# Batch 0 by heads, first weight slices of 128 columns, and a first unit that contracts group 0 first

## The chip, the cores and the metric

The kernel runs on one core of a Trainium2 chip. The core has a matrix engine (PE), a vector engine (DVE), a scalar engine (ACT), a general engine (POOL) and a sync engine (SP). DMAs are issued here from SP's queue, from POOL's queue (the only ones in this kernel that change the type on the way, float32 to bfloat16) and, for two small stores at the end, from ACT's. All of them run on the same 16 DMA engines. Each engine works through its own instructions in the order in which they were written, and the engines wait for each other by semaphores.

The metric is the device time of one execution in microseconds (us). A single execution is also profiled; its trace gives the start and end of each instruction, who waited for whom, and what the DMA engines moved. Times in the trace count from the start of the span. A line number L298 is line 298 of the kernel before.

## The reference

There are 8 batches of 8 heads, each 576 positions by 64, then a gated feed-forward layer over 4608 tokens of 512 features.

```python
# attention without a score matrix
q_s = exp(q); q_s = q_s / sum(q_s, over the 64 features)      # the maxima cancel
k_s = exp(k); k_s = k_s / sum(k_s, over the 576 positions)
kv  = einsum('bhsd,bhse->bhde', k_s, v)                        # 64 x 64 per head
x   = einsum('bhsd,bhde->bhse', q_s, kv)                       # back to 576 x 64 per head
# x: 4608 tokens x 512 (8 heads of 64 side by side)
g   = x @ w_gate                                               # 512 -> 1536
out = (g * sigmoid(g) * (x @ w_val)) @ w_out                   # 1536 -> 512
```

All inputs and the output are float32. The kernel leaves out the maxima and computes in bfloat16 with float32 sums.

## The kernel before, in words

**Tiling.** The 8 heads of a batch are two groups `G` of four heads. One load of `q`, `k` or `v` for one group brings 128 rows with two runs of 2304 bytes each, 576 KB in all; a row holds `T` = 9 positions of two heads. `xt` holds the attention's result, turned so that the 512 features stand on partitions in `KT` = 4 blocks: blocks 0 and 1 come from group 0, blocks 2 and 3 from group 1. The feed-forward layer runs in units `m_unit(c0, n, m)` (L286): for `n` tokens from `c0` and the block `m` of 128 of the 1536 hidden columns it contracts the four blocks of `xt` with `wg` (into `g_ps`), then with `wv` (into `u_ps`); ACT applies Silu to `g_ps` (L305), and DVE multiplies by `u_ps` (L306). `o_mm` (L318) contracts the result with `wo`.

**Order.** The order of the instructions is written out by hand under a manual schedule. Batch 0's attention comes first and has almost nothing beside it. Then the 12 units of batch 0's 576 tokens run (L457), each in two parts of 320 and 256 tokens; after them batch 1's attention runs between the first `o_mm`s, and from then on chunks of 512 tokens go by with the next batch's attention mixed in. PSUM has 8 banks, taken in turn.

**Batch 0's attention** (L354 to L452). SP loads q of group 0, k of group 0, q of group 1, k of group 1 (L355). When k of group 0 has landed, POOL issues v of group 0 as one DMA and v of group 1 as two (positions 0 to 4, then 5 to 8; `BANKS`, L358 to L361), with a change to bfloat16. Then it issues the weights (L380): `wg` and `wv` in turn in slices of columns 0 to 255, 256 to 639, 640 to 1023 and 1024 to 1535, and `wo` in four slices. POOL's DMAs share one queue and start in this order. A unit `m` needs the slice that holds columns 128m to 128m+127, so m = 0 and 1 need the first pair, 2 to 4 the second, 5 to 7 the third, 8 to 11 the fourth. Batch 1's loads on SP wait for the second slice of `wo` (L454).

ACT exponentiates q in two pieces by positions (0 to 4, 5 to 8) and k whole (L373, L124). DVE sums q's exponentials per position and head (`norm_sum`, L138), takes the reciprocal (L143) and multiplies (`norm_mul`, L152). PE turns the result (`turn_pe`, L166); ACT or DVE copies it out (`turn_out`). `key_sum` (L393) sums k's exponentials by matmul, `kv_first` (L404) forms k times v, `scale_first` (L417) scales it by the key sums, `x_mm` (L213) forms x, and `x_out` casts it into `xt`. `spin` (L385) runs matmuls on zeros, which keep PE at work in the lead-in.

In the first unit (`by_part`, L294) PE finishes the first 320 tokens with all four blocks for `g_ps` and `u_ps`, and then does the other 256.

Of the kernel before, what the change touches and what calls it, by code (L numbers as in the profile page):

```python
# [8 lines left out]
FP32 = mybir.dt.float32  # L9
BF16 = mybir.dt.bfloat16  # L10
AF = mybir.ActivationFunctionType
# [4 lines left out]
def kernel(  # L16
# [10 lines left out]
    nc = tc.nc  # L27

    B, H, S, D = q.shape
# [4 lines left out]
    T = S // 64  # L34
    HSTR = S * D
# [11 lines left out]
    def bank(name):  # L47
        return psp.tile([128, 512], FP32, tag="ps", name=name)
# [13 lines left out]

    raw = {}

    def head_ap(src, b, G, t0=0, t1=T):
        return bass.AP(
            tensor=src.tensor,
            offset=src[b, 4 * G].offset + 64 * t0,
            ap=[[T * 64, 128], [2 * HSTR, 2], [1, (t1 - t0) * 64]],
        )  # L70

    def load(what, src, b, G, pieces=((0, T),), after=None):
        t_ = ld.tile([128, 2, T * 64], FP32, tag=what, name=what)
        raw[what, b, G] = t_
        last = None
        for t0, t1 in pieces:
            last = nc.sync.dma_start(out=t_[:, :, 64 * t0:64 * t1], in_=head_ap(src, b, G, t0, t1))
            if after is not None:
                tc.add_manual_dep(last.ins, after.ins.name, SYNC, reason="order of loads")
                after = None  # L80
        return last
# [34 lines left out]

    st = {}

    def exp_of(what, b, G, pieces=((0, T),)):
        s = st.setdefault((b, G), {})  # L120
        e = s["e" + what] = at.tile([128, T, 2, 64], BF16, tag="e" + what, name="e" + what)
        src = raw[what, b, G].rearrange("p h (t d) -> p t h d", d=64)
        for t0, t1 in pieces:
            nc.scalar.activation(out=e[:, t0:t1], in_=src[:, t0:t1], func=AF.Exp)  # L124

    def cast_v(b, G):
        nc.gpsimd.tensor_copy(  # L127
# [1 line left out]
            in_=raw["v", b, G].rearrange("p h (t d) -> p t h d", d=64),  # L129
        )  # L130

    def norm_sum(b, G, pieces=((0, T),)):
        s = st[b, G]
        eq2 = s["eq"].rearrange("p t h d -> p (t h) d")
        rs = at.tile([128, 2 * T], FP32, tag="rs", name="rs")
        first = None
        for t0, t1 in pieces:
            i = nc.vector.reduce_sum(  # L138
                out=rs[:, 2 * t0:2 * t1], in_=eq2[:, 2 * t0:2 * t1, :], axis=mybir.AxisListType.X
            )  # L140
            first = first or i
        rr = s["rr"] = at.tile([128, 2 * T], FP32, tag="rr", name="rr")
        nc.vector.reciprocal(out=rr, in_=rs)  # L143
        return first

    def norm_mul(b, G, pieces=((0, T),), engs=None):
        s = st[b, G]
        eq2 = s["eq"].rearrange("p t h d -> p (t h) d")
        qs = s["qs"] = at.tile([128, T, 128], BF16, tag="qs", name="qs")
        for (t0, t1), eng in zip(pieces, engs or (nc.vector, nc.vector)):  # L150
            n = 2 * (t1 - t0)
            eng.tensor_mul(  # L152
                qs[:, t0:t1, :].rearrange("p t (h d) -> p (t h) d", d=64),
                eq2[:, 2 * t0:2 * t1, :],
                s["rr"][:, 2 * t0:2 * t1].to_broadcast([128, n, 64]),
            )
# [78 lines left out]
    def x_one(b, G):  # L235
        for i in range(2):
            x_out(b, G, i, x_mm(b, G, i))
# [45 lines left out]

    def m_unit(c0, n, m, by_part=False):  # L286
        ms = slice(m * 128, (m + 1) * 128)
        parts = [(c0, n)] if n <= 512 else [(c0, 320), (c0 + 320, n - 320)]
        gu = []
        for nm in ("g_ps", "u_ps"):  # L290
            ps = [bank(nm) for _ in parts]
            gu.append(ps)
        steps = [(a, kk, i) for a in range(2) for kk in range(KT) for i in range(len(parts))]
        if by_part:  # L294
            steps.sort(key=lambda a: (a[2], a[0], a[1]))
        for a, kk, i in steps:
            c, w_ = parts[i]
            nc.tensor.matmul(  # L298
                out=gu[a][i][:, 0:w_], lhsT=(wg, wv)[a][:, kk, ms], rhs=xt[:, kk, c:c + w_],
                start=(kk == 0), stop=(kk == KT - 1),  # L300
            )
        for g_ps, u_ps, (c, w_) in zip(gu[0], gu[1], parts):
            r = c % RING
            sg = ff.tile([128, 512], BF16, tag="sg", name="sg")
            nc.scalar.activation(out=sg[:, 0:w_], in_=g_ps[:, 0:w_], func=AF.Silu)  # L305
            nc.vector.tensor_mul(hr[:, m, r:r + w_], sg[:, 0:w_], u_ps[:, 0:w_])  # L306
# [46 lines left out]
    with tc.manual_schedule():  # L353
        kd = []  # L354
        for G in range(NG):  # L355
            load("q", q, 0, G)
            kd.append(load("k", k, 0, G))
        d = nc.gpsimd.dma_start(out=v16[0], in_=head_ap(v, 0, 0))  # L358
        tc.add_manual_dep(d.ins, kd[0].ins.name, SYNC, reason="order of loads")
        for t0, t1 in BANKS:  # L360
            nc.gpsimd.dma_start(out=v16[1][:, :, 64 * t0:64 * t1], in_=head_ap(v, 0, 1, t0, t1))  # L361

        warm = const.tile([128, 1], FP32, name="warm", tag="warm")
        nc.vector.memset(warm, 0.0)
# [5 lines left out]
        for vb in vbs:  # L370
            nc.vector.memset(vb[:, :, 128:129], 1.0)

        exp_of("q", 0, 0, BANKS)  # L373
        exp_of("k", 0, 0)
        exp_of("q", 0, 1, BANKS)
        first = norm_sum(0, 0, BANKS)
        norm_mul(0, 0, BANKS)
        norm_sum(0, 1, BANKS)

        for c0, n in ((0, 256), (256, 384), (640, 384), (1024, 512)):  # L380
            w_slice(wg, moe_w_gate, c0, n)
            w_slice(wv, moe_w_val, c0, n)
        w_dma = [wo_slice(m0, 3) for m0 in (0, 3, 6, 9)]

        def spin(n, after=None):  # L385
            idle = bank("idle")
            for _ in range(n):
                i = nc.tensor.matmul(out=idle, lhsT=zero[:, 0:128], rhs=zero, start=True, stop=True)  # L388
                if after is not None:
                    tc.add_manual_dep(i.ins, after.ins.name, SYNC, reason="start of the warm-up")  # L390
                    after = None

        def key_sum(G):  # L393
            s = st[0, G]
            ks = bank("ks")
            for t in range(T):
                nc.tensor.matmul(
                    out=ks[:, 0:2], lhsT=s["ek"][:, t, :, :].rearrange("p h d -> p (h d)"), rhs=sel,
                    start=(t == 0), stop=(t == T - 1),
                )  # L400
            s["kvr"] = at.tile([128, 2], FP32, tag="kvr", name="kvr")
            nc.vector.reciprocal(out=s["kvr"], in_=ks[:, 0:2])

        def kv_first(G, t0=0, t1=T):  # L404
            s = st[0, G]
            if t0 == 0:
                s["kv"] = [bank("kv") for _ in range(2)]
            for t in range(t0, t1):
                for g in range(2):
                    r = slice(64 * g, 64 * g + 64)  # L410
                    nc.tensor.matmul(
                        out=s["kv"][g][:, 0:128].rearrange("p (h d) -> p h d", d=64),
                        lhsT=ek_of(0, G, g, t), rhs=v16[G][r, :, 64 * t:64 * t + 64],
                        start=(t == 0), stop=(t == T - 1),
                    )

        def scale_first(G, eng1):  # L417
            s = st[0, G]
            kn = s["kn"] = at.tile([128, 2, 128], BF16, tag="kn1", name="kn1")
            nc.scalar.mul(kn[:, 0, :], s["kv"][0][:, 0:128], s["kvr"][:, 0:1])  # L420
            if eng1 is nc.scalar:
                nc.scalar.mul(kn[:, 1, :], s["kv"][1][:, 0:128], s["kvr"][:, 1:2])
            else:
                nc.vector.tensor_scalar_mul(kn[:, 1, :], s["kv"][1][:, 0:128], s["kvr"][:, 1:2])

        spin(8)
        spin(6, first)
        key_sum(0)
        turn_pe(0, 0, 0)
        turn_pe(0, 0, 1)  # L430
        turn_out(0, 0, 0, nc.scalar)
        exp_of("k", 0, 1)
        turn_out(0, 0, 1, nc.scalar)
        norm_mul(0, 1, BANKS)
        spin(6)
        key_sum(1)
        kv_first(0)
        scale_first(0, nc.scalar)
        turn_pe(0, 1, 0)
        turn_pe(0, 1, 1)  # L440
        turn_out(0, 1, 0, nc.vector)
        turn_out(0, 1, 1, nc.vector)
        xp0 = x_mm(0, 0, 0), x_mm(0, 0, 1)
        kv_first(1, *BANKS[0])
        kv_first(1, *BANKS[1])
        x_out(0, 0, 0, xp0[0], (nc.scalar, nc.scalar))
        x_out(0, 0, 1, xp0[1], (nc.vector, None))
        scale_first(1, nc.vector)
        xp1 = x_mm(0, 1, 0), x_mm(0, 1, 1)
        x_out(0, 1, 0, xp1[0], (nc.scalar, nc.vector))  # L450
        x_out(0, 0, 1, xp0[1], (None, nc.vector))
        x_out(0, 1, 1, xp1[1], (nc.scalar, nc.vector))  # L452

        load_batch(1, w_dma[-3], by_group=True)  # L454
        load_batch(2)

        for m in range(MT):  # L457
            m_unit(0, S, m, by_part=(m == 0))

        exp_of("q", 1, 0)  # L460
        exp_of("k", 1, 0)
# [121 lines left out]
```

The softmax here doesn't subtract the row's maximum and nothing guards it: scores larger than these inputs give would overflow.

## Time and profile before

Five runs took 317.33 to 317.72 us, with a median of 317.46.

| | |
|---|---|
| profiled execution, its own time | 317.2 us |
| its span | 315.3 us |
| granted clock of PE | 1.0 throughout |
| PE busy | 306.7 us (97%), 1894 matmuls |
| DVE, ACT, POOL busy | 163.0, 147.5, 28.1 us |
| PE busy from 0.00 to 6.40 us | 3.60 us, all of it zeros |
| PE busy from 6.40 to 14.40 us (batch 0's attention) | 6.93 us |
| PE busy from 14.40 to 17.04 us (first unit) | 2.31 us |
| PE busy from 17.04 to 38.60 us (the other 11 units) | 21.56 us, all of it |
| DMA's mean rate from 17.04 to 38.60 us | 234 GB/s |

PE is busy almost everywhere after 17 us, so a microsecond that the lead-in loses or wins before that point goes into the whole time, unless a later wait takes it back. For a DMA, the profile gives when it was issued and how long after that it landed. The rate of a DMA that changes the type is counted in the bytes that it writes, half of those that it reads.

### The profile page before, as it was taken

What the parts mean: (1) busy time and instruction counts of PE and PEld (TensorE: products, weight loads), DVE (VectorE), ACT (ScalarE), POOL (GpSimd) and SP (SyncE); (2) the same over time, 40 slices, a digit from 0 to 9 for tenths busy, and PEclk for the clock granted to TensorE, in tenths of its full rate; (3) what the DMA queues carried; (4) which work ended last, traced back from release to release, by engine and by line L of the source; (5) the groups of instructions that cost most, each with busy time, mean ns of one, the idle gap of its engine ahead of it and who ended that gap; (6) DMA issues with size and microseconds to landing.
All of it is one profiled execution on the core that took longest, in us unless ns stands there. A gap on an engine that the chain in (4) does not pass through costs nothing.

```text
span 315.3 us, 4885 instructions
## 1 busy us (share of the span) xinstructions
PE 306.7 (97%) x1894; PEld 152.0 (48%) x1894; DVE 163.0 (52%) x277; ACT 147.5 (47%) x218; POOL 28.1 (9%) x35
## 2 busy tenths in 40 slices
PE   6899999999999999999999999999999999999994
PEld 2477744554444444544454444444454444444443
DVE  3834485784854566455835492639354333423421
ACT  4843488534673475447454737455743113312300
POOL 2920021101100110002000200020000000000000
PEclk9999999999999999999999999999999999999999
DMA  7999999278337815590639153944310202020124
GB/s 275 189 203 207 304 392 389 64 180 338 64 77 201 317 25 119 129 388 2 141 73 377 68 119 64 323 156 104 70 36 0 68 1 67 0 69 5 29 69 102
DMA packets 39305, 45.75 MB, mean 145 GB/s; under 512 B 16369, under 2 KB 23025, under 8 KB 39281
## 3 DMA queue, kind: packets, MB, share of 16 engines
q1 hardware_dynamic: 32480, 39.99, 42.1%
q0 software_dynamic: 6640, 5.31, 10.9%
q8 instruction: 15, 0.25, 0.3%
q10 hardware_dynamic: 160, 0.13, 0.2%
q14 instruction: 10, 0.07, 0.1%
HBM read 37.75 MB, written 9.44 MB: 150 GB/s over the span
## 4 chain that ended last, share of the span: by engine, by line
PE 92%; DMA 3%; ACT 1%; DVE 1%; POOL 1%; issue 0%; SPq 0%
PE g_ps L298 30%; PE u_ps L298 29%; PE o_ps L322 27%; PE kv L191 3%; DMA wv<-in_moe_w_val_dram 2%; DMA k<-in_k_dram 2%; PE xp L267 1%; PE o_ps L342 1%; POOL v L361 0%; DVE qs L152 0%; DVE rs L138 0%; PE tp L166 0%; ACT L124 0%; ACT eq L124 0%; POOL v L358 0%
## 5 line engine op out<-in xcount | busy, mean ns | idle before, releaser
L305 ACT ACTIVATE sg<-g_ps 128x512 bf16<-128x512 f32 (+2 forms) x120 | 65.1, 554 | 138.9 <-PE g_ps L298 131.8
L306 DVE TENSOR_TENSOR hr<-sg,u_ps 128x512 bf16<-128x512 bf16 (+2 forms) x120 | 74.4, 630 | 87.6 <-PE u_ps L298 83.0
L298 PE MATMUL g_ps<-xt,wg 128*128 128x512 bf16 (+2 forms) x480 | 111.6, 358 | 0.2 <-ACT xt L111 0.2
L298 PE MATMUL u_ps<-xt,wv 128*128 128x512 bf16 (+2 forms) x480 | 111.2, 358 | 0.3 <-DMA wv<-in_moe_w_val_dram 0.3
L322 PE MATMUL o_ps<-wo,hr 128*128 128x512 bf16 x420 | 93.6, 379 | 0.0
L298 PEld LDWEIGHTS <-wv 128*128 128x128 bf16 x480 | 46.8, 98 | 47.0 <-DMA wv<-in_moe_w_val_dram 0.6
L298 PEld LDWEIGHTS <-wg 128*128 128x128 bf16 x480 | 45.8, 98 | 45.2 <-issue 0.9
L322 PEld LDWEIGHTS <-hr 128*128 128x128 bf16 x420 | 40.9, 98 | 49.1
L113 DVE COPY o_sb<-o_ps 128x512 f32<-128x512 f32 x33 | 22.4, 680 | 39.2 <-PE o_ps L322 39.2
L127 POOL CAST vb<-v 128x1152 bf16<-128x1152 f32 x14 | 16.1, 1148 | 173.8 <-DMA v<-in_v_dram 85.0
L138 DVE TENSOR_REDUCE rs<-eq 128x18 f32<-128x1152 bf16 (+2 forms) x18 | 21.7, 1215 | 12.7 <-ACT eq L124 12.7
L152 DVE TENSOR_TENSOR qs<-eq,rr 128x1152 bf16<-128x1152 bf16 (+2 forms) x18 | 22.1, 1238 | 0.1
L124 ACT ACTIVATE eq<-q 128x1152 bf16<-128x1152 f32 (+2 forms) x18 | 18.2, 1053 | 4.0 <-DMA q<-in_q_dram 3.9
L124 ACT ACTIVATE ek<-k 128x1152 bf16<-128x1152 f32 x16 | 18.0, 1159 | 0.3 <-DMA k<-in_k_dram 0.2
L305 ACT ACT_TABLE_LOAD x12 | 15.4, 1283 | 0.2
L124 ACT ACT_TABLE_LOAD x11 | 14.1, 1283 | 0.2
L388 PE MATMUL idle<-zero 128*128 128x512 bf16 x20 | 6.5, 480 | 2.8 <-DVE rs L138 1.6
L191 PE MATMUL kv<-vb,ek 64*128 64x129 bf16 x252 | 8.7, 217 | 0.0
L191 PEld LDWEIGHTS <-ek 64*128 64x128 bf16 x252 | 7.3, 94 | 2.7 <-ACT sg L305 2.1
L275 ACT CAST xt<-xp 128x512 bf16<-128x512 f32 x12 | 6.4, 589 | 3.6 <-PE xp L267 3.6
L276 DVE CAST xt<-xp 128x512 bf16<-128x512 f32 x12 | 7.7, 682 | 0.0
L347 ACT COPY o_sb<-o_ps 128x128 f32<-128x128 f32 x2 | 0.5, 266 | 13.3 <-DVE o_sb L346 13.3
(46 smaller groups left out, 70.1 us busy)
## 6 DMA issues: line engine op xcount, KB each, us to landing
q<-in_q_dram SPq DMA_DIRECT2D x16, 576.0 KB, 5.2
k<-in_k_dram SPq DMA_DIRECT2D x16, 576.0 KB, 7.1
out_dram<-o_sb SPq DMA_DIRECT2D x70, 128.0 KB, 2.4
v<-in_v_dram SPq DMA_DIRECT2D x14, 576.0 KB, 8.8
wo<-in_moe_w_out_dram POOLq DMA_DIRECT2D x4, 384.0 KB, 16.8
wg<-in_moe_w_gate_dram POOLq DMA_DIRECT2D x2, 384.0 KB, 9.1
wv<-in_moe_w_val_dram POOLq DMA_DIRECT2D x2, 384.0 KB, 10.1
wg<-in_moe_w_gate_dram POOLq DMA_DIRECT2D x1, 512.0 KB, 13.1
```

Source lines behind the costliest of these rows:

```text
L113: eng.tensor_copy(out=out, in_=in_)
L124: nc.scalar.activation(out=e[:, t0:t1], in_=src[:, t0:t1], func=AF.Exp)
L127: nc.gpsimd.tensor_copy(out=vbs[G][:, :, 0:128].rearrange("p t (h d) -> p t h d", d=64), in_=raw["v", b, G].rearrange("p h (t d) -> p t h ...
L138: i = nc.vector.reduce_sum(out=rs[:, 2 * t0:2 * t1], in_=eq2[:, 2 * t0:2 * t1, :], axis=mybir.AxisListType.X)
L152: eng.tensor_mul(qs[:, t0:t1, :].rearrange("p t (h d) -> p (t h) d", d=64), eq2[:, 2 * t0:2 * t1, :], s["rr"][:, 2 * t0:2 * t1].to_broadca ...
L191: nc.tensor.matmul(out=kv[g][:, c:c + 129], lhsT=ek_of(b, G, g, t), rhs=vbs[G][r, t, 0:129], start=(t == 0), stop=(t == T - 1),)
L276: nc.vector.tensor_copy(out=xt[:, 2 * G + 1, c0:c0 + 512], in_=main[G][1])
L298: nc.tensor.matmul(out=gu[a][i][:, 0:w_], lhsT=(wg, wv)[a][:, kk, ms], rhs=xt[:, kk, c:c + w_], start=(kk == 0), stop=(kk == KT - 1),)
L305: nc.scalar.activation(out=sg[:, 0:w_], in_=g_ps[:, 0:w_], func=AF.Silu)
L306: nc.vector.tensor_mul(hr[:, m, r:r + w_], sg[:, 0:w_], u_ps[:, 0:w_])
L322: nc.tensor.matmul(out=o_ps, lhsT=hr[:, m, r0:r0 + 128], rhs=wo[:, m, :], start=(m == 0), stop=(m == MT - 1),)
L388: i = nc.tensor.matmul(out=idle, lhsT=zero[:, 0:128], rhs=zero, start=True, stop=True)
```

## The change

- `load` and `exp_of` take q of batch 0 head by head: two DMAs of 288 KB for each group in place of one of 576 KB, and two exponentials over 9 positions of one head each, in place of pieces by positions. `norm_sum` sums head by head in the same way.
- v of group 1 comes as one DMA, and `kv_first` of group 1 is one piece.
- The weights' columns are sliced 0 to 127, 128 to 255, 256 to 511, 512 to 1023 and 1024 to 1535: ten DMAs in place of eight.
- The order in the lead-in: `turn_pe` before `key_sum` for group 0, both of group 0's `turn_out`s before k's exponential of group 1, eight matmuls on zeros in place of six, half of group 1's turn before `kv_first(0)`, `scale_first` always on ACT and DVE together, and `x_out` always split between ACT and DVE.
- The first unit does blocks 0 and 1 for all four banks first, then blocks 2 and 3.

```diff
-    def load(what, src, b, G, pieces=((0, T),), after=None):
+    def load(what, src, b, G, after=None, by_head=False):
...
-        for t0, t1 in pieces:
-            last = nc.sync.dma_start(out=t_[:, :, 64 * t0:64 * t1], in_=head_ap(src, b, G, t0, t1))
+        for h in ((0, 1), (1, 2)) if by_head else ((0, 2),):
+            last = nc.sync.dma_start(out=t_[:, h[0]:h[1], :], in_=head_ap(src, b, G, h))
...
-        for t0, t1 in pieces:
-            nc.scalar.activation(out=e[:, t0:t1], in_=src[:, t0:t1], func=AF.Exp)
+        for h in (slice(0, 1), slice(1, 2)) if by_head else (slice(0, 2),):
+            nc.scalar.activation(out=e[:, :, h], in_=src[:, :, h], func=AF.Exp)
...
-        if by_part:
-            steps.sort(key=lambda a: (a[2], a[0], a[1]))
+        if first:
+            steps.sort(key=lambda a: (a[1] // 2, a[2], a[0], a[1]))
...
-        d = nc.gpsimd.dma_start(out=v16[0], in_=head_ap(v, 0, 0))
-        tc.add_manual_dep(d.ins, kd[0].ins.name, SYNC, reason="order of loads")
-        for t0, t1 in BANKS:
-            nc.gpsimd.dma_start(out=v16[1][:, :, 64 * t0:64 * t1], in_=head_ap(v, 0, 1, t0, t1))
+        for G in range(NG):
+            d = nc.gpsimd.dma_start(out=v16[G], in_=head_ap(v, 0, G))
+            if G == 0:
+                tc.add_manual_dep(d.ins, kd[0].ins.name, SYNC, reason="order of loads")
...
-        for c0, n in ((0, 256), (256, 384), (640, 384), (1024, 512)):
+        for c0, n in ((0, 128), (128, 128), (256, 256), (512, 512), (1024, 512)):
             w_slice(wg, moe_w_gate, c0, n)
             w_slice(wv, moe_w_val, c0, n)
...
         spin(8)
         spin(6, first)
+        turn_pe(0, 0, 0)
         key_sum(0)
-        turn_pe(0, 0, 0)
         turn_pe(0, 0, 1)
         turn_out(0, 0, 0, nc.scalar)
+        turn_out(0, 0, 1, nc.scalar)
         exp_of("k", 0, 1)
-        turn_out(0, 0, 1, nc.scalar)
         norm_mul(0, 1, BANKS)
-        spin(6)
+        spin(8)
+        turn_pe(0, 1, 0)
+        kv_first(0)
+        turn_out(0, 1, 0, nc.vector)
+        scale_first(0)
+        turn_pe(0, 1, 1)
         key_sum(1)
-        kv_first(0)
-        scale_first(0, nc.scalar)
-        turn_pe(0, 1, 0)
-        turn_pe(0, 1, 1)
-        turn_out(0, 1, 0, nc.vector)
         turn_out(0, 1, 1, nc.vector)
         xp0 = x_mm(0, 0, 0), x_mm(0, 0, 1)
...
+        x_out(0, 0, 0, xp0[0])
+        kv_first(1)
+        scale_first(1)
+        x_out(0, 0, 1, xp0[1])
+        x_one(0, 1)
...
         for m in range(MT):
-            m_unit(0, S, m, by_part=(m == 0))
+            m_unit(0, S, m, first=(m == 0))
```

More of the change, by code (lines that the diff above doesn't have):

```diff
@@ L63, with head_ap @@
     raw = {}
-    def head_ap(src, b, G, t0=0, t1=T):
+    def head_ap(src, b, G, h=(0, 2)):
         return bass.AP(
             tensor=src.tensor,
-            offset=src[b, 4 * G].offset + 64 * t0,
-            ap=[[T * 64, 128], [2 * HSTR, 2], [1, (t1 - t0) * 64]],
+            offset=src[b, 4 * G + 2 * h[0]].offset,
+            ap=[[T * 64, 128], [2 * HSTR, h[1] - h[0]], [1, T * 64]],
         )
-    def load(what, src, b, G, pieces=((0, T),), after=None):
+    def load(what, src, b, G, after=None, by_head=False):
         t_ = ld.tile([128, 2, T * 64], FP32, tag=what, name=what)
@@ L117, with exp_of @@
     st = {}
-    def exp_of(what, b, G, pieces=((0, T),)):
+    def exp_of(what, b, G, by_head=False):
         s = st.setdefault((b, G), {})
@@ L130, in cast_v, with norm_sum, norm_mul @@
         )
-    def norm_sum(b, G, pieces=((0, T),)):
+    def norm_sum(b, G, by_head=False):
         s = st[b, G]
-        eq2 = s["eq"].rearrange("p t h d -> p (t h) d")
-        rs = at.tile([128, 2 * T], FP32, tag="rs", name="rs")
+        rs = at.tile([128, T, 2], FP32, tag="rs", name="rs")
         first = None
[L137 to L140, printed above, removed]
+        for h in (slice(0, 1), slice(1, 2)) if by_head else (slice(0, 2),):
+            i = nc.vector.reduce_sum(out=rs[:, :, h], in_=s["eq"][:, :, h, :], axis=mybir.AxisListType.X)
             first = first or i
         rr = s["rr"] = at.tile([128, 2 * T], FP32, tag="rr", name="rr")
-        nc.vector.reciprocal(out=rr, in_=rs)
+        nc.vector.reciprocal(out=rr, in_=rs.rearrange("p t h -> p (t h)"))
         return first
-    def norm_mul(b, G, pieces=((0, T),), engs=None):
+    def norm_mul(b, G, pieces=((0, T),)):
         s = st[b, G]
@@ L149, in norm_mul @@
         qs = s["qs"] = at.tile([128, T, 128], BF16, tag="qs", name="qs")
-        for (t0, t1), eng in zip(pieces, engs or (nc.vector, nc.vector)):
+        for t0, t1 in pieces:
             n = 2 * (t1 - t0)
-            eng.tensor_mul(
+            nc.vector.tensor_mul(
                 qs[:, t0:t1, :].rearrange("p t (h d) -> p (t h) d", d=64),
@@ L282, in x_both, with m_unit @@
             )
-    def m_unit(c0, n, m, by_part=False):
+    def m_unit(c0, n, m, first=False):
         ms = slice(m * 128, (m + 1) * 128)
@@ L355 @@
         for G in range(NG):
-            load("q", q, 0, G)
+            load("q", q, 0, G, by_head=True)
             kd.append(load("k", k, 0, G))
-        d = nc.gpsimd.dma_start(out=v16[0], in_=head_ap(v, 0, 0))
-        tc.add_manual_dep(d.ins, kd[0].ins.name, SYNC, reason="order of loads")
-        for t0, t1 in BANKS:
-            nc.gpsimd.dma_start(out=v16[1][:, :, 64 * t0:64 * t1], in_=head_ap(v, 0, 1, t0, t1))
+        for G in range(NG):
+            d = nc.gpsimd.dma_start(out=v16[G], in_=head_ap(v, 0, G))
+            if G == 0:
+                tc.add_manual_dep(d.ins, kd[0].ins.name, SYNC, reason="order of loads")
         warm = const.tile([128, 1], FP32, name="warm", tag="warm")
@@ L371 @@
             nc.vector.memset(vb[:, :, 128:129], 1.0)
-        exp_of("q", 0, 0, BANKS)
+        exp_of("q", 0, 0, True)
         exp_of("k", 0, 0)
-        exp_of("q", 0, 1, BANKS)
-        first = norm_sum(0, 0, BANKS)
+        exp_of("q", 0, 1, True)
+        first = norm_sum(0, 0, True)
         norm_mul(0, 0, BANKS)
-        norm_sum(0, 1, BANKS)
-        for c0, n in ((0, 256), (256, 384), (640, 384), (1024, 512)):
+        norm_sum(0, 1, True)
+        for c0, n in ((0, 128), (128, 128), (256, 256), (512, 512), (1024, 512)):
             w_slice(wg, moe_w_gate, c0, n)
@@ L402, in key_sum, with kv_first @@
             nc.vector.reciprocal(out=s["kvr"], in_=ks[:, 0:2])
-        def kv_first(G, t0=0, t1=T):
+        def kv_first(G):
             s = st[0, G]
-            if t0 == 0:
-                s["kv"] = [bank("kv") for _ in range(2)]
-            for t in range(t0, t1):
+            s["kv"] = [bank("kv") for _ in range(2)]
+            for t in range(T):
                 for g in range(2):
@@ L415, in kv_first, with scale_first @@
                     )
-        def scale_first(G, eng1):
+        def scale_first(G):
             s = st[0, G]
@@ L420, in scale_first @@
             nc.scalar.mul(kn[:, 0, :], s["kv"][0][:, 0:128], s["kvr"][:, 0:1])
[L421 to L424, printed above, removed]
+            nc.vector.tensor_scalar_mul(kn[:, 1, :], s["kv"][1][:, 0:128], s["kvr"][:, 1:2])
         spin(8)
         spin(6, first)
+        turn_pe(0, 0, 0)
         key_sum(0)
-        turn_pe(0, 0, 0)
         turn_pe(0, 0, 1)
         turn_out(0, 0, 0, nc.scalar)
+        turn_out(0, 0, 1, nc.scalar)
         exp_of("k", 0, 1)
-        turn_out(0, 0, 1, nc.scalar)
         norm_mul(0, 1, BANKS)
-        spin(6)
-        key_sum(1)
-        kv_first(0)
-        scale_first(0, nc.scalar)
-        turn_pe(0, 1, 0)
-        turn_pe(0, 1, 1)
-        turn_out(0, 1, 0, nc.vector)
+        spin(8)
[4 more added lines that the diff above has]
+        turn_pe(0, 1, 1)
+        key_sum(1)
         turn_out(0, 1, 1, nc.vector)
         xp0 = x_mm(0, 0, 0), x_mm(0, 0, 1)
[L444 to L452, printed above, removed]
+        x_out(0, 0, 0, xp0[0])
[3 more added lines that the diff above has]
+        x_one(0, 1)
         load_batch(1, w_dma[-3], by_group=True)
```

## The prediction

> **What bounds the kernel now.** I read the busy shares first, then PE in order of time through the lead-in, then the landing of each weight slice, then the rate of the DMA engines. The page's busy table gives the frame:
>
> ```profile
> PE 306.7 (97%) x1894; PEld 152.0 (48%) x1894; DVE 163.0 (52%) x277; ACT 147.5 (47%) x218; POOL 28.1 (9%) x35
> ```
>
> PE is the bound, and all that the change touches lies before 25 us. So the question is when PE gets into its even step of units, and whether anything stops it there later. PE in order of time (start, length, what it does; in brackets its idle time and what ended it):
>
> ```profile
> 12.36 0.61 PE L220 MATMUL xp<-qt,kn 64*64 64x320 bf16 x8
> 12.90 0.68 PE L411 MATMUL kv<-v,ek 64*128 64x128 bf16 x18
> 14.03 0.45 PE L220 MATMUL xp<-qt,kn 64*64 64x320 bf16 x8 [0.46 <-DVE kn L424]
> ...
> 15.62 0.72 PE L298 MATMUL u_ps<-xt,wv 128*128 128x320 bf16 x4 [0.30 <-DMA wv<-in_moe_w_val_dram]
> 16.17 0.60 PE L298 MATMUL g_ps<-xt,wg 128*128 128x256 bf16 x4
> 16.61 0.60 PE L298 MATMUL u_ps<-xt,wv 128*128 128x256 bf16 x4
> 17.04 1.14 PE L298 MATMUL g_ps<-xt,wg 128*128 128x320 bf16 x8
> ...
> 22.92 1.14 PE L298 MATMUL g_ps<-xt,wg 128*128 128x320 bf16 x8
> 23.90 1.14 PE L298 MATMUL u_ps<-xt,wv 128*128 128x320 bf16 x8
> 24.88 1.14 PE L298 MATMUL g_ps<-xt,wg 128*128 128x320 bf16 x8
> 25.86 1.14 PE L298 MATMUL u_ps<-xt,wv 128*128 128x320 bf16 x8
> ```
>
> From 17.04 a unit takes 1.96 us (0.98 for `g_ps`, 0.98 for `u_ps`) without a gap. The first unit began at 14.41 and ended at 17.04, 2.63 us: 0.67 us of it is waiting, for x of group 1 and for the first `wv` slice. Counting on, m = 4 begins at 22.92 and reads `wv` from 23.90; m = 5 reads `wv` from 25.86. These two times decide what follows.
>
> The DMA issues give size and time from issue to landing, here for the first `wg`, the first `wv` and the third `wv` slice (columns 640 to 1023):
>
> ```profile
> wg<-in_moe_w_gate_dram POOLq DMA_DIRECT2D x1, 256.0 KB, 5.4
> ```
> ```profile
> wv<-in_moe_w_val_dram POOLq DMA_DIRECT2D x1, 256.0 KB, 6.0
> ```
> ```profile
> 12.48 0.79 POOL L99 DMA_DIRECT2D wv<-in_moe_w_val_dram  x1
> ```
> ```profile
> wv<-in_moe_w_val_dram POOLq DMA_DIRECT2D x1, 384.0 KB, 11.3
> ```
>
> They were issued at 8.79, 9.54 and 12.48, so they landed at 14.2, 15.5 and 23.8. The last is needed at 25.86: 2.1 us to spare. The DMA engines' packets (one per run of columns) in the single microseconds from 9, 12, 19, 26 and 63:
>
> ```profile
> DMA packets 177, 0.20 MB, mean 197 GB/s; under 512 B 5, under 2 KB 177, under 8 KB 177
> ```
> ```profile
> DMA packets 372, 0.19 MB, mean 188 GB/s; under 512 B 5, under 2 KB 372, under 8 KB 372
> ```
> ```profile
> DMA packets 272, 0.21 MB, mean 205 GB/s; under 512 B 5, under 2 KB 272, under 8 KB 272
> ```
> ```profile
> DMA packets 206, 0.21 MB, mean 210 GB/s; under 512 B 1, under 2 KB 206, under 8 KB 206
> ```
> ```profile
> DMA packets 815, 0.21 MB, mean 209 GB/s; under 512 B 815, under 2 KB 815, under 8 KB 815
> ```
>
> The first is v. The next three are slices of 256, 384 and 512 columns, written as packets of 512, 768 and 1024 bytes; the last is a transposing DMA inside the chip, in packets of 256 bytes. The weight stream is never idle up to 36 us, so a slice lands when the bytes and packets ahead of it are through; when POOL issues it hardly matters. A slice is 512 packets whatever its width: 1.38 us at 256 columns (512/372), 1.88 at 384, 2.49 at 512.
>
> **The change, part by part.**
>
> *Attention of batch 0 (all estimates from the trace's durations).* Halves of q let the first exponential start when the first 288 KB are in, some 0.8 us before the 4.78 of now; the second waits for the same landing as now, and of 576 elements per row it takes about 0.67 us (mean of 736 ns for 640 and 612 ns for 512). Thus q's exponentials end near 5.45 instead of 6.03, and DVE's sums, reciprocals and products come 0.6 to 0.75 us earlier for both groups. That gain doesn't pass on whole: `kv_first(0)` needs v of group 0, landed at 10.7 (issued 6.51, 4.2 to land), and goes at about 10.9 instead of 11.14. `scale_first` on two engines instead of ACT twice saves another 0.2: `x_mm` of group 0 at 12.0 (now 12.36). `kv_first(1)` follows at 12.5 (now 12.90), if its v is in; `x_mm` of group 1 at 13.6 (now 14.03); the first unit at 14.05 (now 14.41). The other moves cost nothing there: two more matmuls on zeros (0.43 us) end near 10.0, with group 1's products due at 10.55; group 0's second `turn_out`, now ahead of k's exponential on ACT, lets that start near 9.5, and k landed at 9.37 (issued 2.27, 7.1 to land); SP's two extra issues, 0.5 us each, delay k of group 1, whose packets run only after q's, from about 7 us.
>
> *First unit.* With blocks 0 and 1 first, PE has 0.98 us of work that needs x of group 0 alone, while group 1's casts (four of 0.38 to 0.49 us on two engines) finish by 14.8. If the first pair of slices is in, the unit takes 1.96 us and ends at 16.0: 1.0 us earlier than now. The Silu table load (1.28 us) ends by about 16.0 and holds up no PE work, since the banks of m = 0 are next needed at m = 2.
>
> *v of group 1 in one DMA.* Its two pieces landed 2.0 us after group 0's (8.1 + 4.6 against 6.51 + 4.2). As 256 packets like group 0's, 0.295 MB written at 197 GB/s, it takes 1.5: everything behind it gains 0.5.
>
> *Slices.* Up to the end of the third `wv` slice the stream was 2 x 1.38 + 4 x 1.88 = 10.28 us. Now it is four slices of 128 columns, 2 x 1.38 and 2 x 2.49 = 7.74, plus 4d, where d is the time of 512 packets of 256 bytes. No DMA of the trace shows d. From below: 0.63 us, the transposes' 815 packets per us, which is also the byte rate of the widest slices. From above: 1.38, as long as a slice of twice the width. A straight line through 2.49, 1.88 and 1.38 gives 0.88, but the rate in bytes falls already, 210, 205, 188, more at each step. The nearest row is the 256-column slice, the same queue and cast, so I go above the line, to the middle: **d = 1.0**. Change of the stream: 4.0 + 7.74 - 10.28 - 0.50 = +0.96 us (bounds -0.5 and +2.5).
>
> The first pair lands in time (14.2 - 0.5 - 0.4 = 13.3, and 15.5 - 0.5 - 0.8 = 14.2). But the new third wide slice holds columns 512 to 1023, and PE wants it at m = 4, no longer at m = 5. It lands at 23.8 + 0.96 = **24.75**; PE would want it at 16.0 + 3 x 1.96 + 0.98 = 22.9, so PE stands still about 1.9 us there, and `u_ps` of m = 4 starts 0.85 later than the 23.90 of now. Behind this wait ACT and DVE only wait along. The earlier microsecond is therefore lost, and so is any error of the attention's estimate up to 1.9 us. POOL's issue of that slice comes near 13.5, far ahead of its packets; it now waits for v of group 1 to land (12.2), which costs nothing for the same reason.
>
> *Afterwards.* The fourth pair follows in 2 x 2.49 us, needed 7.8 us later. Batch 1's loads wait for the second `wo` slice and shift by the same 0.96; its first q is read at 39.74 and landed at 38.25 (issued 32.95, 5.3 to land), and both shift alike. PE has no slack later to win it back.
>
> **Sum:** +0.85 us. The profiled execution took 317.2 around its span of 315.3, 0.26 under the median of 317.46; it becomes 318.05, and the median **318.3**. What this kernel's runs can tell from no change is about 0.2%, 0.63 us.
>
> [...]
>
> **The rivals.**
>
> *Packets cost only their bytes.* For it: 205 to 210 GB/s from 768 bytes up, and the transposes. Against it: 188 at 512. With d from 0.63 to 0.88 the sum is -0.6 to +0.4. This is the one that ends on the other side: the same wait, at m = 4 for `wv`, decides, and below d = 0.79 the kernel is faster; at 0.63 by 0.6 us, 316.8.
>
> *Small packets take as long as those of twice the size, or longer.* For it: the fall at 512 bytes. Against it: from 768 to 512 the time per packet still fell by a quarter. From d = 1.25: +1.85; at 1.38, +2.4, 319.8.
>
> *No wait at m = 4 at all*, so that the gain of the first unit stays: -1.0, 316.4. The stream would have to be 1.9 us shorter than I have it; even d = 0.63 gives only 1.5.
>
> *The attention by heads is late.* It costs only beyond the 1.9 us that the wait covers; nothing in the trace comes near.
>
> **How the numbers follow.** Forecast (d 0.88 to 1.25, +0.4 to +1.85): 50%. Bytes only: 25%. Long packets: 17%. No wait: 5%. Late attention: 3%. Faster by over 0.2%: no wait and the very end of bytes only, 0.08. Within 0.2%: most of bytes only and the forecast below d = 0.95, 0.33. Slower: 0.59. The range, 317.1 to 319.9, runs from d = 0.70 to d = 1.40 and leaves out a tenth on each side.
>
> **What would show it.** Right: the first unit ends by 16.5; PE waits for DMA `wv` at m = 4 for 1 to 3 us, ending near 24.75; about 500 packets per us while the narrow slices run; an earlier end of q's sums that moves nothing. Wrong: no DMA wait on PE after 17 us, packets over 700 per us, or a first unit that ends later than now.

## The result and the profile after

| | before | changed |
|---|---|---|
| median | 317.51 us (43 runs) | 319.39 us (24 runs) |
| lowest to highest | 317.11 to 318.94 | 317.06 to 322.19 |
| profiled execution, span | 317.2, 315.3 | 317.24, 315.3 |

The changed kernel is slower: ratio 1.0056, with an interval of 1.0041 to 1.0071, about 1.8 us. The ratio leaves out the two longest executions of the changed kernel (322.03 and 322.19), which lie over 1.5% above its fastest. The middle half of its executions spans 2.4 us, against 0.5 before, and the profiled one is among its fastest. So this profile shows the mechanism of the waits, but not the loss; that needed a profile of a typical execution, which the first experiment brought.

The page's busy table of the profiled execution is nearly that of before:

```profile
PE 306.8 (97%) x1896; PEld 152.1 (48%) x1896; DVE 163.3 (52%) x278; ACT 147.3 (47%) x217; POOL 28.8 (9%) x36
```

PE in order of time, with the instructions that answer to those shown of before, and behind them what the weight loads (PEld) waited for up to 60 us: us in total, times, longest:

```profile
11.40 0.45 PE L163 MATMUL tp<-ident,qs 128*128 128x128 bf16 x5 [1.51 <-DVE qs L149]
...
13.05 0.44 PE L217 MATMUL xp<-qt,kn 64*64 64x320 bf16 x8
13.42 0.68 PE L407 MATMUL kv<-v,ek 64*128 64x128 bf16 x18
14.55 0.45 PE L217 MATMUL xp<-qt,kn 64*64 64x320 bf16 x8 [0.45 <-DVE kn L417]
14.94 0.45 PE L295 MATMUL g_ps<-xt,wg 128*128 128x320 bf16 x2
...
16.91 1.14 PE L295 MATMUL g_ps<-xt,wg 128*128 128x320 bf16 x8
...
22.79 1.14 PE L295 MATMUL g_ps<-xt,wg 128*128 128x320 bf16 x8
24.07 1.15 PE L295 MATMUL u_ps<-xt,wv 128*128 128x320 bf16 x8
```
```profile
PEld L295 <- DMA wv<-in_moe_w_val_dram: 0.4, 1, 0.4
```

The first unit runs without a gap, 14.94 to 16.91, in 1.97 us, as forecast (1.96). But it starts later than before (14.41), where I had 14.05, and ends 0.13 us earlier than before, where I had 1.0. From 22.79 to 24.07 `g_ps` of m = 4 takes 1.28 us in place of 0.98: 0.30 us of standing still for `wv`, in the place that the prediction named, and `u_ps` starts 0.17 us later than before (24.07 against 23.90).

The DMA rate in the microsecond from 13, when only the narrow slices run, then the issues of group 0's and group 1's v and of the `wv` slice for m = 4 to 7 (size, time to landing; issued at 6.38, 7.24 and 13.63):

```profile
DMA packets 720, 0.18 MB, mean 178 GB/s; under 512 B 720, under 2 KB 720, under 8 KB 720
```
```profile
v<-in_v_dram POOLq DMA_DIRECT2D x1, 288.0 KB, 5.5
```
```profile
v<-in_v_dram POOLq DMA_DIRECT2D x1, 288.0 KB, 6.1
```
```profile
wv<-in_moe_w_val_dram POOLq DMA_DIRECT2D x1, 512.0 KB, 10.4
```

720 packets of 256 bytes per us make a 128-column slice 0.71 us, less than my 1.0. v, on the other hand, landed at 11.9 and 13.35, where before it was there at 10.7 and 12.7, and I had counted on 10.7 and 12.2. The slice itself landed at 24.03, forecast 24.75.

### The profile page after: what moved, and what is told of

Its sections match the earlier page's. It is cut to its first block, busy times and chain, and to the rows that moved or that the text cites. A ratio compares the mean times of both kernels' runs of the same rounds, so it can differ in the third digit from the quotient of the medians.

```text
span 315.3 us, 4893 instructions
## 1 busy us (share of the span) xinstructions
PE 306.8 (97%) x1896; PEld 152.1 (48%) x1896; DVE 163.3 (52%) x278; ACT 147.3 (47%) x217; POOL 28.8 (9%) x36
## 3 DMA queue, kind: packets, MB, share of 16 engines
q0 software_dynamic: 7424, 5.31, 11.2%
## 4 chain that ended last, share of the span: by engine, by line
PE 89%; DMA 7%; ACT 1%; DVE 1%; issue 0%; POOL 0%; SPq 0%
PE g_ps L295 28%; PE u_ps L295 28%; PE o_ps L319 27%; DMA wv<-in_moe_w_val_dram 3%; PE kv L188 3%; DMA v<-in_v_dram 2%; DMA k<-in_k_dram 1%; PE xp L264 1%; PE o_ps L339 1%; DVE qs L149 0%; DVE rs L137 0%; PE tp L163 0%; ACT L124 0%; ACT eq L124 0%; POOL v L356 0%
## 5 line engine op out<-in xcount | busy, mean ns | idle before, releaser
L137 DVE TENSOR_REDUCE rs<-eq 128x18 f32<-128x1152 bf16 (+1 forms) x18 | 21.8, 1215 | 12.6 <-ACT eq L124 12.6
L124 ACT ACTIVATE eq<-q 128x1152 bf16<-128x1152 f32 (+1 forms) x18 | 18.4, 1054 | 3.1 <-DMA q<-in_q_dram 2.9
## 6 DMA issues: line engine op xcount, KB each, us to landing
wg<-in_moe_w_gate_dram POOLq DMA_DIRECT2D x2, 512.0 KB, 10.7
wv<-in_moe_w_val_dram POOLq DMA_DIRECT2D x2, 512.0 KB, 12.2
```

Of the source, the lines that this page charges most:

```text
L124: nc.scalar.activation(out=e[:, :, h], in_=src[:, :, h], func=AF.Exp)
L137: i = nc.vector.reduce_sum(out=rs[:, :, h], in_=s["eq"][:, :, h, :], axis=mybir.AxisListType.X)
```

## Experiments

Each was timed over several executions beside the kernel before on the same chip. In the first four the kernel before had a median of 317.41, in the next four 317.52, in the last four 317.50. The last four ran on another chip than the first eight.

### 1. The changed kernel again

No edit.

> The changed kernel itself, once more, to see a second profile of it and how its executions scatter. Wait theory (the third wide wv slice lands late, PE stands still at m = 4): the granted clock is 1.0 and the time follows the landing of that slice, 317.2 to 319. Clock theory (PE has too little work before group 1's turn, where it waits 1.5 us for qs, so in some executions its granted clock falls for some microseconds): the executions' mean clock lies between 0.987 and 1.0, and each 0.01 of it costs about 3.2 us; the slowest are those of the lowest clock, up to 322.

321.12 us (318.99 to 322.22, 6 runs), ratio 1.0101 [1.0072, 1.0130]. The mean granted clock was 0.987, 0.987, 0.988, 0.988, 0.994 and 1.0, the last in the shortest execution; those of the kernel before lay at 0.997 or above. That is the clock theory's forecast. The profile is now of a typical execution (321.12, span 319.2). ACT's exponential of k of group 0, first in the kernel before, then here, and PE:

```profile
6.23 1.16 ACT L124 ACTIVATE ek<-k 128x1152 bf16<-128x1152 f32 x1 [0.20 <-DMA k<-in_k_dram]
```
```profile
7.29 1.16 ACT L124 ACTIVATE ek<-k 128x1152 bf16<-128x1152 f32 x1 [2.24 <-DMA k<-in_k_dram]
```
```profile
11.69 0.45 PE L163 MATMUL tp<-ident,qs 128*128 128x128 bf16 x5 [0.83 <-DVE qs L149]
...
14.82 1.14 PE L407 MATMUL kv<-v,ek 64*128 64x128 bf16 x18 [1.16 <-DMA v<-in_v_dram]
16.42 0.71 PE L217 MATMUL xp<-qt,kn 64*64 64x320 bf16 x8 [0.46 <-DVE kn L417]
17.06 0.71 PE L295 MATMUL g_ps<-xt,wg 128*128 128x320 bf16 x2
...
20.87 1.37 PE L295 MATMUL g_ps<-xt,wg 128*128 128x320 bf16 x8
```

And its busy times by stretch, where the number after POOL's is PE's granted clock:

```profile
5.30:14.40 9.10, 6.11 (x76) 3.27 (x74) 7.04 (x15) 5.23 (x8) 6.78 (x9) 1.00 1.04 222
14.50:21.30 6.80, 6.02 (x44) 3.77 (x45) 2.11 (x6) 3.43 (x7) 4.80 (x7) 0.50 1.44 188
21.40:40.00 18.60, 18.60 (x154) 14.85 (x153) 7.57 (x19) 6.62 (x19) 0.37 (x1) 1.00 1.20 228
```

Two losses can be read here. k of group 0 is exponentiated at 7.29, not at 6.23 as before; v waits for that landing to be issued at all; group 1's v holds PE up until 14.82 (before: 12.90). And from 14.5 to 21.3 the matrix engine ran at half its clock: the first unit takes 3.81 us in place of 1.96. PE's 18 matmuls of `kv` took 1.14 us in place of 0.68. No wait for `wv` is left at m = 4 here, because PE is later than the slice. The trace's clock record has the half clock for 6.83 us in this execution. In the other three profiles with a fall (runs 3, 11 and 12) it lasts 3.41, 3.41 and 6.83 us, and the four falls come at different times: 14.49 here, then 13.28, 7.57 and 14.75. PE was not idle in the 3.41 us before the fall here: it was busy for 1.97 us between 11.07 and 14.49, and its longest gap was 1.2 us.

### 2. More matmuls on zeros

```diff
         norm_mul(0, 1, BANKS)
-        spin(8)
+        spin(14)
         turn_pe(0, 1, 0)
```

> The changed kernel with 14 instead of 8 matmuls on zeros before group 1's turn, 1.3 us more, which fills PE's 1.5 us of waiting. Clock theory: the granted clock stays at 1.0 in nearly every execution and the median falls from 319.4 to 317.5 or 318. Wait theory: PE waits at m = 4 as before, the median stays near 319.

319.21 us (318.31 to 319.85, 8 runs), ratio 1.0048 [1.0031, 1.0064]; the clock was at 0.997 or above in all eight. Beside it the changed kernel had 321.12 (six executions), and 319.39 in the 24 of the result, so what goes with the clock is 0.2 to 1.9 us by these medians. Among those 24, the 13 executions with a clock of 0.997 or above have a median of 318.64, the other 11 one of 321.14; they may differ in more than the clock. The clock recovers, as the clock theory said, but its 317.5 to 318 was missed: 1.8 us over the kernel before remain. The wait theory's 319 came true for another reason. In this run's profile PE waits for v of group 0 until 13.23, and the first unit starts at 16.45; the wait at m = 4 is again 0.3 us. So most of the rest is neither that wait nor the clock, but late v.

### 3. The old slices in the changed kernel

```diff
-        for c0, n in ((0, 128), (128, 128), (256, 256), (512, 512), (1024, 512)):
+        for c0, n in ((0, 256), (256, 384), (640, 384), (1024, 512)):
```

> The changed kernel with the column slices of the kernel before (256, 384, 384, 512), all else changed. Wait theory: no wait for wv after the first unit, so the first unit's gain stays and the median is 316.5 to 317.2. Clock theory: the clock scatters as in the changed kernel (0.987 to 1.0), since the lead-in on PE is the same; the median stays 1 us or more above 317.5, near 318.5.

319.89 us (317.76 to 320.89, 8 runs), ratio 1.0070 [1.0046, 1.0095], clocks from 0.988 to 1.0. The wait theory's 316.5 to 317.2 fell. The first unit starts at 17.78, since v of group 0 lands at 13.4 and PE waits for it. So most of the loss isn't in the slices.

### 4. The new slices in the kernel before

```diff
-        for c0, n in ((0, 256), (256, 384), (640, 384), (1024, 512)):
+        for c0, n in ((0, 128), (128, 128), (256, 256), (512, 512), (1024, 512)):
```

> The kernel before with the new column slices (128, 128, 256, 512, 512), nothing else. Wait theory: with 0.74 us for a slice of 128 columns (as the profile of the changed kernel shows) the third wide wv slice lands about 24.2 and PE waits for it at m = 4, +0.3 us, up to +1.5 in executions where it lands later. Clock theory: the lead-in on PE is that of the kernel before, so the clock stays at 1.0 and nothing of the scatter up to 322 appears: 317.5 to 318.2.

317.96 us (317.42 to 318.49, 12 runs), ratio 1.0012 [1.0001, 1.0022], clocks from 0.997. This is the prediction's own mechanism by itself. In its profile the first unit ends at 16.47, 0.57 us earlier than before, and all of that goes at m = 4:

```profile
22.35 1.14 PE L298 MATMUL g_ps<-xt,wg 128*128 128x320 bf16 x8
23.90 1.15 PE L298 MATMUL u_ps<-xt,wv 128*128 128x320 bf16 x8 [0.41 <-DMA wv<-in_moe_w_val_dram]
```

`u_ps` starts at 23.90, to the hundredth as before. This profile is of the fastest execution (317.42), in which wait and gain cancel; the median is half a microsecond longer. So the mechanism is there. That the wait is longer in the other executions, and makes up the 0.5 us, is likely but not shown.

### 5. q by heads in the kernel before

```diff
-            load("q", q, 0, G)
+            load("q", q, 0, G, by_head=True)     # two DMAs, one head's run of each row in each
```

> The kernel before with one thing changed: q of batch 0 loaded head by head, two DMAs of 288 KB per group (the exponentials stay by positions). Head theory (six loads in place of four make k of group 0, or v behind it, land later on the slowest DMA engine): v of group 0 lands after 11.5 in place of 10.7, the matmuls of k times v start late, and the median rises to 318 to 320, with executions whose clock falls. Whole-v theory (it is v of group 1 as one DMA that delays v): nothing of this, 317.4 within 0.3.

319.45 us (317.17 to 321.62, 12 runs), ratio 1.0062 [1.0037, 1.0087], with clocks down to 0.987 in the three longest. This one edit gives as much loss (1.93 us) and as much scatter (middle half 2.6 us) as the whole change, and the head theory's forecast holds. The DMA engines' packets from 5 to 6 us, first in the kernel before, then here:

```profile
DMA packets 184, 0.39 MB, mean 387 GB/s; under 512 B 16, under 2 KB 16, under 8 KB 184
```
```profile
DMA packets 118, 0.24 MB, mean 237 GB/s; under 512 B 15, under 2 KB 15, under 8 KB 118
```

The queue isn't short of issued loads then: all six, 2.4 MB, had been issued by 3.6 us. Nor do the DMA engines stand idle: their busy share is 1.04 before and 1.13 here, so a packet took some 150 ns in place of 90. The stream falls to 0.6 of its rate, k of group 0 is first read at 7.28, and PE follows:

```profile
11.95 0.38 PE L402 MATMUL ks<-sel,ek 128*128 128x2 bf16 x9 [1.26 <-ACT ek L129]
12.98 0.68 PE L416 MATMUL kv<-v,ek 64*128 64x128 bf16 x18 [0.65 <-DMA v<-in_v_dram]
...
15.85 0.45 PE L225 MATMUL xp<-qt,kn 64*64 64x320 bf16 x8 [0.45 <-DVE kn L429]
16.23 0.90 PE L303 MATMUL g_ps<-xt,wg 128*128 128x320 bf16 x4
```

The first unit starts at 16.23 in place of 14.41. In the changed kernel's own two profiles the same microsecond moved 251 and 260 GB/s, in runs 2 and 3 it moved 336 and 309, and in the seven profiles with q whole 362 to 401. The dip alone doesn't say when k lands: ACT reads k of group 0 at 6.05 to 6.30 with q whole, at 6.10 in the fast profile of the result in spite of its dip, and at 6.78 to 7.98 in the other five with q by heads.

### 6. q whole in the changed kernel

```diff
-            load("q", q, 0, G, by_head=True)
+            load("q", q, 0, G)
```

> The changed kernel with q of batch 0 loaded whole again, two runs in one DMA (the exponentials stay by head). Head theory: v of group 0 lands near 10.7 again, the clock stays at 1.0 and the median falls from about 320 to 317.3 to 318.2; what is left over the kernel before is the wait for wv at m = 4, 0.3 to 0.5 us. Whole-v theory: v lands as late as in the changed kernel, median 319 or more.

317.87 us (317.50 to 318.89, 11 runs), ratio 1.0009 [1.0000, 1.0019], clock 1.0 in every execution. This is the counterpart of the last: from 5 to 6 us the rate is 378 GB/s, v of group 0 lands at 10.77. What is left over the kernel before is 0.35 us, with a wait for `wv` at m = 4 (until 24.57) and v of group 1 landing at 13.8. The head theory's forecast holds.

### 7. q whole and the old slices in the changed kernel

```diff
-            load("q", q, 0, G, by_head=True)
+            load("q", q, 0, G)
...
-        for c0, n in ((0, 128), (128, 128), (256, 256), (512, 512), (1024, 512)):
+        for c0, n in ((0, 256), (256, 384), (640, 384), (1024, 512)):
```

> The changed kernel with q loaded whole and the column slices of the kernel before. Head theory together with the wait theory: neither late v nor a wait at m = 4 is left, so the new order of the lead-in and the new first unit show what they are worth: 316.5 to 317.2. Whole-v theory: 318.5 or more.

318.33 us (317.71 to 319.04, 12 runs), ratio 1.0020 [1.0011, 1.0029]. A miss: without the wait at m = 4 it is slower, not faster, than with it, and the median lies between the two theories' ranges. The old first `wv` slice lands late, and the first unit stops for it:

```profile
15.41 0.45 PE L295 MATMUL g_ps<-xt,wg 128*128 128x320 bf16 x2
16.45 0.44 PE L295 MATMUL u_ps<-xt,wv 128*128 128x320 bf16 x2 [0.60 <-DMA wv<-in_moe_w_val_dram]
```

Here the narrow slices win 0.46 us (317.87 against 318.33), while in the kernel before they lose 0.5. That their sign depends on how late v, ahead of them in the queue, leaves the DMA engines would fit both, but no run isolates it.

### 8. v of group 1 whole in the kernel before

```diff
-        for t0, t1 in BANKS:
-            nc.gpsimd.dma_start(out=v16[1][:, :, 64 * t0:64 * t1], in_=head_ap(v, 0, 1, t0, t1))
+        nc.gpsimd.dma_start(out=v16[1], in_=head_ap(v, 0, 1))
```

> The kernel before with one thing changed: v of group 1 as one DMA. Whole-v theory: v of group 0 or of group 1 lands 1 us or more later than before (10.7 and 12.7), median 318 or more. Head theory: v of group 1 lands at 12.2 to 12.7, and the median stays within 0.3 of 317.4.

318.12 us (317.75 to 318.43, 11 runs); all eleven lie above the median of the kernel before, though the interval of the ratio, 1.0007 [0.9996, 1.0019], still reaches 1. The median is in the whole-v theory's range. In its profile v of group 1, issued at 7.18, landed at 13.45 (6.3 us), against 12.68 before. One DMA in place of two is later, not earlier. In the changed order it is the same: 13.83 in run 6 with one DMA, 13.0 in run 9 with two. In this profile PE never waits for v itself, but the first `wv` slice behind it is late too, and the first unit, which before went on at 15.62, stops for it:

```profile
16.37 0.72 PE L298 MATMUL u_ps<-xt,wv 128*128 128x320 bf16 x4 [0.45 <-DMA wv<-in_moe_w_val_dram]
```

The microsecond from 10 to 11 moved 123 GB/s, against 168 before, though the packets are larger; why, no run shows.

### 9 and 10. Two mixtures

The ninth is the changed kernel with q whole, v of group 1 in two DMAs and milder slices; the tenth is the kernel before with these slices and the first unit's new order.

```diff
-            load("q", q, 0, G, by_head=True)
+            load("q", q, 0, G)
...
-            d = nc.gpsimd.dma_start(out=v16[G], in_=head_ap(v, 0, G))
+                for t0, t1 in BANKS:      # group 1 alone
+                    nc.gpsimd.dma_start(out=v16[G][:, :, 64 * t0:64 * t1], in_=ap)
...
-        for c0, n in ((0, 128), (128, 128), (256, 256), (512, 512), (1024, 512)):
+        for c0, n in ((0, 128), (128, 128), (256, 384), (640, 384), (1024, 512)):
```
```diff
-        for c0, n in ((0, 256), (256, 384), (640, 384), (1024, 512)):
+        for c0, n in ((0, 128), (128, 128), (256, 384), (640, 384), (1024, 512)):
...
-            steps.sort(key=lambda a: (a[2], a[0], a[1]))
+            steps.sort(key=lambda a: (a[1] // 2, a[2], a[0], a[1]))
```

> The changed kernel with q loaded whole, v of group 1 in two DMAs as before, and slices of 128, 128, 384, 384 and 512 columns, so that the third wide slice is needed at m = 5 again. If the three terms add up as in the runs so far (heads, whole v and the wait at m = 4 each cost, the order of the lead-in and the first unit gain): v of group 1 lands near 12.7, no wait for wv after the first unit, 316.6 to 317.2. If the new order gains nothing by itself: 317.4 or more.

> The kernel before with slices of 128, 128, 384, 384 and 512 columns and the first unit's new order (blocks 0 and 1 first), the attention untouched. Wait theory: the first unit loses its wait for wv (0.5 us) and for group 1's casts, and nothing waits at m = 4: 316.6 to 317.0. If the slices' two extra DMAs cost as much as they win: 317.4.

317.81 us (ratio 1.0010 [1.0000, 1.0020]) and 317.78 us (1.0002 [0.9986, 1.0018]). Neither beats the kernel before, so the terms don't add up as the ninth's first forecast had it, and the wait theory's 316.6 to 317.0 for the tenth fell. The ninth also shows what the new order of the lead-in does with q whole and v in two DMAs. Its first unit starts at 14.66, later than before (14.41). Group 1's first turn, which now stands ahead of `kv_first(0)`, waits 0.36 us for `qs` until 11.24, so that `kv_first(0)` starts at 11.62 in place of 11.14. Even so the first unit ends at 16.63, 0.4 us early, and then the next pair of slices is not there:

```profile
19.08 1.15 PE L295 MATMUL g_ps<-xt,wg 128*128 128x320 bf16 x8 [0.33 <-DMA wg<-in_moe_w_gate_dram]
20.96 1.15 PE L295 MATMUL u_ps<-xt,wv 128*128 128x320 bf16 x8 [0.73 <-DMA wv<-in_moe_w_val_dram]
```

The tenth stops in the same unit, m = 2, for `wv`, until 20.35. In the kernel before, that slice is there at 19.9 (issued 11.01, 8.9 us) and is used at 19.98. In these profiles the weight stream is just fast enough for the start that PE has in the kernel before, so an earlier end of the first unit is given back at the next slice.

### 11. q in two DMAs by partitions

```diff
+            for p in (0, 64):
+                ap = bass.AP(tensor=src.tensor, offset=src[b, 4 * G].offset + p * T * 64, ap=[[T * 64, 64], [2 * HSTR, 2], [1, T * 64]])
+                last = nc.sync.dma_start(out=t_[p:p + 64, :, :], in_=ap)
```

> The kernel before with q of batch 0 loaded in two DMAs of 64 partitions each, both runs of a row in each, so the number of loads is that of the load by heads, but not their shape. If the number of loads in flight is what breaks the stream: the rate falls from 5 to 6 us as in the load by heads (237 to 260 GB/s in place of 371 to 387), k of group 0 lands near 7, the median is 318.5 or more. If it is the shape, one contiguous head per DMA: no dip, k at 6.2, 317.4 within 0.4.

320.24 us (319.67 to 323.13, 6 runs), ratio 1.0099 [1.0072, 1.0127]. From 5 to 6 us 290 GB/s; k of group 0 was in use only after 9 us. So the loss doesn't need the shape of one head per DMA. But SP took about 0.65 us for each issue here, k's included, not 0.47, so this run mixes a slower issue with the number of loads and doesn't show that the number alone does it.

### 12. Only group 0 by heads

```diff
-            load("q", q, 0, G, by_head=True)
+            load("q", q, 0, G, by_head=(G == 0))
```

> The kernel before with q of group 0 alone loaded head by head, group 1 whole: five loads in place of four. If the split of group 0 ahead of k is what delays k: k of group 0 lands at 6.8 to 7.3 and the median is 318.5 or more. If it is the split of group 1, or six loads: k at 6.2 and the median 317.4 within 0.4, perhaps 0.2 less, since the first exponentials can't use the earlier half here.

320.39 us (319.60 to 321.71, 6 runs), ratio 1.0094 [1.0076, 1.0112]. From 5 to 6 us 242 GB/s, and k of group 0, issued at 1.67, landed 6.3 us later, at 8.0, beyond the 6.8 to 7.3 that was expected; this profile is of the longest execution. The split of the one load ahead of k is enough. What in the queue makes two DMAs ahead of k slow the stream is open; group 1's split isn't needed for it.

## Why the prediction was right, and where it wasn't

Direction and range held: slower, 319.39 inside 317.1 to 319.9. The forecast of +0.85 us was half of what was measured (1.8 to 1.9), and its sum was made of terms that erred in both directions. That the number fell inside the range is in part luck: the wait on which the forecast rests is worth 0.3 to 0.5 us, and the main loss is late attention, a rival that I gave 3%. My own signs say the same. Of those for right, PE's wait at m = 4 came, but with 0.3 us in place of 1 to 3, and the first unit ended at 16.91, not by 16.5. Of those for wrong, two came: 720 packets per us, and, in the typical execution of run 1, a first unit that ends at 20.87, later than the 17.04 of before.

- **The wait at m = 4 for `wv`: right in place, too large.** It shows in the changed kernel's profile (0.30 us), alone in the kernel before (0.41 us in a profile without net loss; the run's median is +0.5 us) and with q whole (that run's median is +0.35 us over the kernel before). I had PE standing still 1.9 us and +0.85 net; in the changed kernel's profile `u_ps` of m = 4 starts 0.17 us later than before.
- **d, the time of a 128-column slice: too high.** 1.0 taken, 0.71 measured, between the lower bound (0.63) and the straight line (0.88); four slices cost 1.2 us less. The rate fell from 188 to 178 GB/s in the last halving, less than in the one before, so "more at each step" was wrong. Half the bytes in as many packets took about half the time, 0.71 us against 1.38.
- **v of group 1 in one DMA: wrong in sign.** Forecast 0.5 us earlier; alone it lands 0.8 us later. The step took group 0's steady rate for the whole DMA, but that rate didn't hold: 123 GB/s from 10 to 11 us in run 8. The errors in d and in v have opposite signs; the slice landed at 24.03 where I had 24.75.
- **The attention: wrong.** The sentence that failed is that SP's extra issues delay only k of group 1, with group 0's k and v landing as before. In a typical execution k of group 0 lands 1 us later, v is issued behind it and lands later still, and `x_mm` of group 1 comes at 16.42 where I had 13.6. That is beyond the 1.9 us of cover. "The attention by heads is late" was the rival that I gave 3% because nothing in the trace came near; the two runs that only split q (5 and 12) show that it is the main term, +1.9 and +2.9 us. "The other moves cost nothing there" failed too: group 1's first products, due at 10.55, reached PE only at 11.2 (runs 3 and 9) to 11.7 (run 1), and with the new order `kv_first(0)` stands behind them.
- **The granted clock: missing from the prediction.** It was 1.0 in the profile of before, and I took it as given. The record of the clock begins only at 5.19 us there; ahead of it the eight matmuls on zeros took 3.60 us, 0.45 each, against 0.25 in the six after it. In the profiles of runs 1, 3, 11 and 12 the clock was at half for 3.41 or 6.83 us. With PE's wait filled with zeros (run 2) it stayed at 0.997 or above in all eight executions, and the median was 0.2 to 1.9 us lower. What lets it fall isn't settled.
- **The first unit with blocks 0 and 1 first: right.** 1.97 us without a gap; but the tenth run, which has it with narrower first slices, gains nothing by it, since the next slices aren't there.
- **What decides the sum.** By the medians of the single edits, heads give +1.9, the slices +0.5 and whole v +0.6 in the kernel before, the last with an interval that reaches 0. They don't add up to the 1.9 of the whole change: in run 1, PE that is late from v no longer waits for `wv`.

## What to carry to other kernels

A load that is split so that its first half arrives earlier can make the loads behind it later, so look first at what is queued behind it: here the half of q came 1 us earlier, and k and v of group 0 came up to 1.8 and 3 us later in the runs with q by heads. Where a stream of weights paces the first units, an earlier start can be taken back at the next slice, as the 0.57 us of run 4 were; the slack of every slice has to be read, not only that of the one that the change moves. And a profile of one execution may be a lucky one: where the runs scatter more than before, look at a second profile and at the clock before explaining the median.

## What the runs showed of the hardware that I had not expected

- Two DMAs of 288 KB in place of one of 576 KB ahead of k lowered the rate from 5 to 6 us: 237 to 336 GB/s in the six profiles with that split by heads, 362 to 401 in the seven with q whole. The packets took longer (in run 5 some 150 ns in place of 90); the engines did not stand idle.
- 256 KB read in 512 packets that are written as 256 bytes each took 0.71 us, 178 GB/s written against 188 for packets of 512 bytes.
- v of 576 KB in one DMA landed 0.8 us later than in two, in each of two pairs of profiles (13.45 against 12.68, 13.83 against 13.0).
- PE at half clock for 6.83 us cost the first unit 1.85 us, in the profile of run 1. What lets the clock fall is not PE's busy sum alone: from 5.3 to 14.4 us it was 6.1 us there and 4.7 in run 12, which fell, but 5.5 in run 5, whose clock stayed. The 3.41 us ahead of the four falls (runs 11, 3, 12 and 1) held 0.41, 0.94, 1.48 and 1.97 us of PE's work, while those from 8.35 to 11.77 us in the profile of the result held 1.91 and the clock stayed at 1.0.
- The granted clock of an execution can read 1.0 though PE began slowly. In runs 6, 7 and 8 the six matmuls on zeros from 6.24 us took 2.74 us in place of 1.47, and the mean clock of these three profiles reads 1.0, 0.997 and 1.0; the record of the clock begins there only at 9.0 to 10.6 us.
